# An attention and GLU block rewritten: row-tiled scores, column-tiled values, exponentials shared with VectorE, and a list-scheduled order

## Chip, core and metric

The kernel runs on one core of a Trainium2 chip. The metric is the device time of one execution in microseconds (us), measured on the chip; a profile of one such execution gives the traces quoted below. Before the change the median of two runs was 1394.49 us (1393.20 to 1395.78). Five engines matter: TensorE (PE, its weight loads PEld), ScalarE (ACT), VectorE (DVE), GpSimd (POOL) and SyncE (SP), which only issues DMA here. The record sorts runs into a fast and a slow state (slow: over 1.5% above the fastest run of the same kernel).

## The reference, cut to what matters

```python
# S = 2048 rows, D = 640, H = 32 heads of Dh = 20, F = 1728, all bf16
h  = x + attention(layernorm(x)) @ wo        # softmax over 2048 keys, no mask
h2 = h + ((layernorm(h) @ w_gate) * (layernorm(h) @ w_up)) @ w_down
```

Attention needs 32 x 2048 x 2048 exponentials, which is 1,048,576 per partition of a 128-partition engine. A head has only 20 features. So a score matmul contracts over 20 of the 128 rows that its tile takes in the kernel before (the traces list the tile as 128*128 there), and a value matmul fills only some 20 of its 128 columns.

## The kernel before

It ran in three stages, one after the other: LayerNorm and projections; attention, head by head; then wo, the second LayerNorm and the GLU. The core of the attention loop (cuts marked):

```python
for h in range(H):
    for qh in range(QH):                       # two halves of 1024 queries
        acc = acps.tile([P, QW], F32, name="acc")          # one accumulator (bufs=1)
        for kt in range(NT):                   # 16 blocks of 128 keys
            scr_ = scps.tile([P, QW], F32, name="sc")
            for c in range(QW // 512):
                nc.tensor.matmul(scr_[:, c*512:(c+1)*512],
                                 lhsT=kpad[:, kt*P:(kt+1)*P],   # 20 rows of keys, 108 of zeros
                                 rhs=qpad[:, c*512:(c+1)*512], start=True, stop=True)
            E = epool.tile([P, QW], BF16, name="E")
            nc.scalar.activation(E[:], scr_[:], ACT.Exp, scale=sm_scale)
            for c in range(QW // 512):
                nc.tensor.matmul(acc[:, c*512:(c+1)*512],
                                 lhsT=vext[kt][:, vb:vb+P],     # 20 value columns, ones, padding
                                 rhs=E[:, c*512:(c+1)*512], start=(kt == 0), stop=(kt == NT-1))
        # ... cut: eviction of acc, the sums to DRAM and back, scaling ...
```

The softmax here doesn't subtract the row's maximum and nothing guards it: scores larger than these inputs give would overflow.

## Time and profile before

| stage | us of the span | what fills it |
|---|---|---|
| before the first exponential | 0 to 119 | loads, LayerNorm, projections |
| attention | 119 to 1131 | ScalarE and TensorE, both nearly full |
| after the last exponential | 1131 to 1393 | wo, LayerNorm, GLU on TensorE |

These are lines of the profile page of the kernel before: busy time by engine, the chain of work that ended last, and the two costliest groups (line, engine, operation, tiles, shapes, count, then busy us and mean ns of one, then the engine's idle time before them and its releaser).

```profile
span 1392.9 us, 15855 instructions
PE 1248.1 (90%) x5704; PEld 533.9 (38%) x5704; DVE 372.0 (27%) x593; ACT 1031.3 (74%) x1235; POOL 186.5 (13%) x228
ACT 62%; PE 20%; issue 8%; DMA 4%; DVE 4%; SPq 2%; POOL 0%; ACTq 0%; DVEq 0%
...
L355 ACT ACTIVATE E<-sc 128x1024 bf16<-128x1024 f32 x1024 | 945.8, 1070 | 66.7 <-PE acc L357 66.7
L347 PE MATMUL sc<-qpad,kpad 128*128 128x512 bf16 x2048 | 611.8, 379 | 22.5 <-ACT E L355 20.5
```

The chain is 62% ScalarE, nearly all exponentials. The 66.7 us of idle time before them are the changes of head: a new unit must wait until the one accumulator has been evicted.

The chain in order of time, in the kernel before, shows the pitch (start, duration, what):

```profile
133.26 0.87 ACT E L355
134.12 0.05 issue
134.17 0.87 ACT E L355
135.04 0.05 issue
```

One exponential of 1024 columns starts every 0.91 us. TensorE spends four 512-column matmuls on it. The timeline of the kernel before shows how closely matmuls follow each other:

```profile
1340.12 0.38 PE L514 MATMUL psy<-Wd_9630,hh_10968 128*128 128x512 bf16 x1
1340.33 0.22 PE L521 MATMUL psy<-Wd_9630,hh_10968 128*128 128x128 bf16 x1
```

A 512-column matmul lasts 0.38 us, but the next one starts after 0.21 us (5153 times at full clock in this trace: 215 ns both at the least and in the median). So four take 0.86 us and TensorE is almost as full as ScalarE. A busy share from the 0.38 us would overstate it: one reads TensorE by starts, not by durations.

### The profile page before, as it was taken

What the parts mean: (1) busy time and instruction counts of PE and PEld (TensorE: products, weight loads), DVE (VectorE), ACT (ScalarE), POOL (GpSimd) and SP (SyncE); (2) the same over time, 40 slices, a digit from 0 to 9 for tenths busy, and PEclk for the clock granted to TensorE, in tenths of its full rate; (3) what the DMA queues carried; (4) which work ended last, traced back from release to release, by engine and by line L of the source; (5) the groups of instructions that cost most, each with busy time, mean ns of one, the idle gap of its engine ahead of it and who ended that gap; (6) DMA issues with size and microseconds to landing.
All of it is one profiled execution on the core that took longest, in us unless ns stands there. A gap on an engine that the chain in (4) does not pass through costs nothing.

```text
span 1392.9 us, 15855 instructions
## 1 busy us (share of the span) xinstructions
PE 1248.1 (90%) x5704; PEld 533.9 (38%) x5704; DVE 372.0 (27%) x593; ACT 1031.3 (74%) x1235; POOL 186.5 (13%) x228
## 2 busy tenths in 40 slices
PE   3888999999999999999999999999999953999998
PEld 2433333333333333333333333333333321444443
DVE  8342000420230132004102300410143226453422
ACT  5405999999999999999999999999999941221311
POOL 4223111111111111121111111112111000000000
PEclk9998999999999999999999999999999987999999
DMA  6752000100010001001000100100010144211100
GB/s 164 59 113 48 9 8 8 31 18 9 8 37 8 11 20 25 8 8 33 17 8 9 37 10 8 25 20 8 13 35 10 43 139 129 68 61 40 38 20 19
DMA packets 106258, 48.18 MB, mean 35 GB/s; under 512 B 85956, under 2 KB 97156, under 8 KB 106180
## 3 DMA queue, kind: packets, MB, share of 16 engines
q1 hardware_dynamic: 100088, 39.53, 11.9%
q0 software_dynamic: 4960, 5.78, 2.8%
q10 hardware_dynamic: 1132, 1.87, 0.6%
q8 instruction: 45, 0.74, 0.2%
q14 instruction: 33, 0.27, 0.1%
HBM read 20.40 MB, written 5.51 MB: 19 GB/s over the span
## 4 chain that ended last, share of the span: by engine, by line
ACT 62%; PE 20%; issue 8%; DMA 4%; DVE 4%; SPq 2%; POOL 0%; ACTq 0%; DVEq 0%
ACT E L355 61%; PE psg L494 4%; PE psu L485 4%; PE psy L514 4%; PE acc L357 2%; PE sc L347 2%; DVE qtmp L220 1%; PE psy L521 1%; PE psqk L212 1%; SPq L233 1%; PE psoA L454 1%; PE psv L182 1%; DVE rc L284 0%; SPq L442 0%; DVE lnstats L84 0%
## 5 line engine op out<-in xcount | busy, mean ns | idle before, releaser
L355 ACT ACTIVATE E<-sc 128x1024 bf16<-128x1024 f32 x1024 | 945.8, 1070 | 66.7 <-PE acc L357 66.7
L347 PE MATMUL sc<-qpad,kpad 128*128 128x512 bf16 x2048 | 611.8, 379 | 22.5 <-ACT E L355 20.5
L347 PEld LDWEIGHTS <-kpad 128*128 128x128 bf16 x2048 | 196.5, 96 | 251.9 <-issue 15.7
L365 DVE COPY cst<-acc 52x1024 f32<-52x1024 f32 x64 | 77.9, 1217 | 743.0 <-PE acc L357 743.0
L502 ACT COPY gsb<-psg 128x512 f32<-128x512 f32 (+1 forms) x56 | 32.8, 586 | 107.6 <-PE psg L494 107.4
L329 POOL MEMSET qpad<- 128x1024 bf16 x64 | 60.9, 952 | 358.2 <-issue 358.2
L325 POOL MEMSET kpad<- 128x2048 bf16 x32 | 57.8, 1805 | 369.1 <-PE sc L347 346.7
L357 PE MATMUL acc<-E,vx_102 128*128 128x512 bf16 x128 | 38.4, 381 | 37.7 <-ACT E L355 37.7
L284 DVE RECIPROCAL rc<-Dcol 8x1024 f32<-8x1024 f32 (+1 forms) x9 | 58.9, 6544 | 18.9 <-DMA Dcol<-cst 18.9
L355 ACT ACT_TABLE_LOAD x1 | 1.3, 1283 | 55.4 <-PE sc L347 55.4
L357 PE MATMUL acc<-E,vx_100 128*128 128x512 bf16 x128 | 38.3, 381 | 1.5 <-ACT E L355 1.5
L357 PE MATMUL acc<-E,vx_101 128*128 128x512 bf16 x128 | 38.5, 383 | 0.0
L357 PE MATMUL acc<-E,vx_114 128*128 128x512 bf16 x128 | 37.9, 377 | 0.3 <-ACT E L355 0.3
L357 PE MATMUL acc<-E,vx_115 128*128 128x512 bf16 x128 | 37.9, 377 | 0.3 <-ACT E L355 0.3
L357 PE MATMUL acc<-E,vx_103 128*128 128x512 bf16 x128 | 37.9, 377 | 0.0
L357 PE MATMUL acc<-E,vx_107 128*128 128x512 bf16 x128 | 37.9, 377 | 0.0
L357 PE MATMUL acc<-E,vx_109 128*128 128x512 bf16 x128 | 37.9, 377 | 0.0
L357 PE MATMUL acc<-E,vx_110 128*128 128x512 bf16 x128 | 37.9, 377 | 0.0
L357 PE MATMUL acc<-E,vx_106 128*128 128x512 bf16 x128 | 37.9, 377 | 0.0
L357 PE MATMUL acc<-E,vx_108 128*128 128x512 bf16 x128 | 37.9, 377 | 0.0
L357 PE MATMUL acc<-E,vx_111 128*128 128x512 bf16 x128 | 37.9, 377 | 0.0
L357 PE MATMUL acc<-E,vx_113 128*128 128x512 bf16 x128 | 37.9, 377 | 0.0
(808 smaller groups left out, 1383.3 us busy)
## 6 DMA issues: line engine op xcount, KB each, us to landing
rbt<-rscr SPq DMA_DIRECT2D x64, 80.0 KB
out_dram<-ot SPq DMA_DIRECT2D x16, 160.0 KB
Dcol<-cst SPq DMA_DIRECT2D x64, 4.0 KB
on_70<-cst POOLq DMA_DIRECT2D x16, 40.0 KB, 2.1
on_71<-cst POOLq DMA_DIRECT2D x16, 40.0 KB, 2.1
on_72<-cst POOLq DMA_DIRECT2D x16, 40.0 KB, 2.1
on_73<-cst POOLq DMA_DIRECT2D x16, 40.0 KB, 2.1
qT_85<-qtmp POOLq DMA_DIRECT2D x6, 80.0 KB, 3.1
```

The source lines that it names most:

```text
L182: nc.tensor.matmul(ps[:, 0:512], lhsT=lnT[c][:, t * P:(t + 1) * P], rhs=Wv[c][:, 0:512], start=(c == 0), stop=(c == KT - 1),)
L284: nc.vector.reciprocal(rc[r0:r0 + bs_, :], Dcol[r0:r0 + bs_, :])
L325: nc.gpsimd.memset(kpad[:], 0.0)
L329: nc.gpsimd.memset(qpad[:], 0.0)
L347: nc.tensor.matmul(scr_[:, c * 512:(c + 1) * 512], lhsT=kpad[:, kt * P:(kt + 1) * P], rhs=qpad[:, c * 512:(c + 1) * 512], start=True, stop ...
L355: nc.scalar.activation(E[:], scr_[:], ACT.Exp, scale=sm_scale)
L357: nc.tensor.matmul(acc[:, c * 512:(c + 1) * 512], lhsT=vext[kt][:, vb:vb + P], rhs=E[:, c * 512:(c + 1) * 512], start=(kt == 0), stop=(kt ...
L365: nc.vector.tensor_copy(cst[0:52, :], acc[0:52, :])
L485: nc.tensor.matmul(psu[0:M, :], lhsT=Wu[c][:, f * P:f * P + M], rhs=ln2T[c][:, ch * 512:(ch + 1) * 512], start=(c == 0), stop=(c == KT - 1),)
L494: nc.tensor.matmul(psg[0:M, :], lhsT=Wg[c][:, f * P:f * P + M], rhs=ln2T[c][:, ch * 512:(ch + 1) * 512], start=(c == 0), stop=(c == KT - 1),)
L502: nc.scalar.copy(gsb[0:M, :], psg[0:M, :])
L514: nc.tensor.matmul(psy[:, 0:512], lhsT=hh[f][0:K, tt * P:(tt + 1) * P], rhs=Wd[f][0:K, 0:512], start=(f == 0), stop=(f == NFT - 1),)
```

## The change

The intent is to remove both limits and the serial stages:

1. Scores use 32-row tiles. Four heads lie on partitions 0, 32, 64 and 96, and their four matmuls are meant to run at the same time.
2. Values use 32-column tiles in the same way: four heads accumulate into four quarters of one tile of 512 columns in PSUM, the pool that the kernel's matmuls write to (such a tile is called a bank here).
3. About 18% of the exponentials move to VectorE. It computes `A*s + B` into uint16, and the bits, read as bf16, are a piecewise-linear exponential. Three more copies shifted by constants (27, 55, 94) even out the error. The value matmul adds up all four, so each such block costs four value matmuls.
4. The order of every instruction comes from a list scheduler in the kernel's own Python: projections, wo and GLU ("background jobs") go into the gaps of attention. The order of each engine's instructions is then part of the program.

```diff
-                        nc.tensor.matmul(scr_[...], lhsT=kpad[:, kt*P:(kt+1)*P], rhs=qpad[...], start=True, stop=True)
+                    nc.tensor.matmul(bank[:, n * cw:(n + 1) * cw],
+                                     lhsT=KTt[32 * j:32 * j + Dh, g, kt * P:(kt + 1) * P],
+                                     rhs=QTt[32 * j:32 * j + Dh, g, 0:cw], start=True, stop=True, ...)
-                            lhsT=vext[kt][:, vb:vb + P],
+            nc.tensor.matmul(ACC[32 * j:32 * j + 32, 0:cw], lhsT=VX[:, kt, h * VS:h * VS + 32], rhs=ap,
+                             start=(n == 0), stop=last, tile_position=(0, 32 * j), ...)
-                    nc.scalar.activation(E[:], scr_[:], ACT.Exp, scale=sm_scale)
+                nc.scalar.activation(st["e"][eslot["i"]][:, 0:n * 512], src[:, 0:n * 512], ACT.Exp, scale=SCALE)
+            p_ = add("DVE", ..., lambda e: nc.vector.tensor_scalar(
+                YT[ys["i"]][:, 0, :], bank, scalar1=EXP_A, scalar2=EXP_B, op0=ALU.mult, op1=ALU.add), ...)
+            s1 = s_op(1, 0, SH[1], "DVE", [p_])
+            s2 = s_op(2, 0, SH[2], "DVE", [p_])
+            s3 = s_op(3, 2, SH[3] - SH[2], "POOL", [s2])
+    NON = 10                                         # slots for attention outputs, 8 per chunk of queries
+    CHUNKS = [(0, 512), (512, 512), (1024, 512), (1536, 256), (1792, 256)]
+            mu = add("POOL", ..., lambda e: nc.gpsimd.tensor_tensor(
+                ON[:, on_of[ci, g], 0:cw], a[:, 0:cw], BC[0][:, 0:cw], ALU.mult), ..., gate=lambda: bool(on_free) and ...)
# ... cut: LayerNorm, jobs, the scheduler's loop (some 900 lines) ...
```

## The prediction

> What bounds it now. The span is 1392.9 us. The chain that ended last is 62% ScalarE exponentials, and the ScalarE timeline shows three stages: about 118 us before the first exponential, 1045 us of attention, and about 230 us of output projection and GLU after it. In attention an exponential (128x1024) lasts 1.07 us and starts every 0.917 us, about 0.064 us more than its 1024 columns at 0.833 ns. Every 16 of them cost another 1 to 2 us where the single accumulator waits for its eviction (the waits view: 66.7 us of ScalarE idle for acc). TensorE is almost as full: four 512-column matmuls per exponential, issued about 0.216 us apart, use only 20 of 128 rows (scores) or 52 of 128 columns (values). VectorE is 27% and GpSimd 13% busy.
>
> What changes, with counts from the ordered instruction streams:
> - ScalarE keeps 859,000 of 1,049,000 exponential columns per partition, in 672 instructions of mostly 1536 or 1024 columns. At 0.833 ns plus 0.064 us each that is about 760 us, down from 945 busy.
> - The other 18% go to VectorE as 370 PSUM passes (a 512-column PSUM cast lasts 0.68 us in this trace) and 740 bf16-sized SBUF adds (about 0.2 us, from 0.30 us start to start for the 640-column subtraction), plus 370 adds on GpSimd. VectorE then totals about 600 us: not a bound.[...]
> - TensorE. [...]tiled work (scores 437, values 674, q/k 171 us) would fall to a quarter, 320 us, at perfect four-way overlap; I allow 360, as many score bursts hold only two or three row tiles. Untiled work (values projection, dense q, wo, GLU) is about 250 us. The stream changes tiling mode 1586 times[...]. A 512-column matmul lasts 0.38 us against 0.216 pitch[...]. Sum: 785 to 870 us.
> - Projections, wo and GLU, serial today (about 350 us outside attention), move into gaps inside attention. Outside remain a head of about 25 us (loads, first LayerNorm) and a tail of about 55 us after the last value matmul (243 GLU, 112 down, 32 wo matmuls, one LayerNorm with its transposes).
>
> Critical path. TensorE (about 830 us) and ScalarE (about 760 us) are nearly balanced, and TensorE idles for about 30 us in head and tail. With some 5% lost to waits between them I expect 905 us, a gain of 35%. The range is 850 to 985 us. Chances: faster 0.985, same 0.01, slower 0.005.
>
> What would show it. Right: first exponential before 35 us; ScalarE busy about 800 us (durations overlap), idle mainly waiting for TensorE scores; the chain led by TensorE with ScalarE second; VectorE about 65%; last exponential to end about 60 us; granted clock near 1.0. Wrong: ScalarE above 93% busy during attention ([...]the time nearer 850), or TensorE packed while score or value matmuls of different tiles start more than 0.08 us apart (tiling overlaps worse, time over 950).
>
> What would make it wrong: [...]weight loads of 32-column tiles not hidden; 256-column tiled matmuls limited by issue; VectorE and GpSimd blocking each other so that their share of scores arrives late[...]; the granted clock falling.

Its TensorE sum came to 785 to 870 us: 360 for tiled work, about 250 for untiled work and 175 to 260 for the 1586 mode changes. That last term was the estimate of 0.11 to 0.16 us a change, whose upper figure is the duration of 0.38 us less the pitch of 0.216. The streaming terms count 2.4 columns per ns; the measured 512 columns in 215 ns are 2.38. The 0.833 ns per column of an exponential could not be read from the kernel before, where all exponentials have 1024 columns; the changed kernel's trace gives it (1536 and 1024 columns start 1.331 and 0.904 us apart).

## The result, and the profile after

The changed kernel took 978.91 us, the median of two runs (973.92 and 983.91), and 982.50 us (four runs, 976.87 to 988.34) when it was run again with later experiments (e5). The ratio to the kernel before is 0.702 (95% interval 0.694 to 0.711). Ratios here are the mean time of one kernel's fast runs over that of the other's of the same rounds, so they are not quite the ratios of the medians quoted.

The same parts of the page for the changed kernel, with the rows of 40 equal slices (each digit is a busy share in tenths; PEclk is the granted TensorE clock):

```profile
span 972.1 us, 23682 instructions
PE 865.9 (89%) x9543; PEld 384.7 (40%) x9543; DVE 663.7 (68%) x1743; ACT 782.2 (80%) x727; POOL 288.1 (30%) x419
PE   0889888898999799999999999999999999678968
ACT  0679789696899799999999999999999999306501
PEclk9999999897999899999999999999999999979989
PE 59%; ACT 20%; DVE 11%; issue 6%; DMA 3%; SPq 0%; POOL 0%; ACTq 0%; DVEq 0%; POOLq 0%
...
L932 ACT ACTIVATE EA<-SA 128x1536 bf16<-128x1536 f32 x340 | 505.8, 1488 | 58.5 <-PE D L858 29.9
L932 ACT ACTIVATE EB<-SB 128x1024 bf16<-128x1024 f32 x332 | 354.0, 1066 | 49.2 <-PE ACC L998 47.2
L952 DVE TENSOR_SCALAR Y<-D 128x512 uint16<-128x512 f32 x370 | 254.2, 688 | 145.2 <-PE SA L858 90.4
L962 DVE TENSOR_SCALAR Y<-Y 128x512 uint16<-128x512 uint16 x740 | 199.6, 307 | 6.9
```

ScalarE's exponentials went from 945.8 us busy to about 860 by durations, of which some overlap. The chain is led by TensorE now. The ACT row shows three parts: slices 2 to 14 with 6 to 9 tenths, a stretch from slice 15 to 34 at nine tenths throughout, and then a hole (a 3 and a 0) followed by a short second burst. The waits view of the changed kernel (engine and line, whom it waited for: us in total, times, longest us) says what the hole is:

```profile
ACT EB L932 <- PE ACC L998: 47.2, 1, 47.2
POOL ON L1043 <- PE D L605: 45.9, 1, 45.9
ACT EA L932 <- PE D L858: 29.9, 15, 6.6
ACT EA L932 <- PE SA L858: 26.5, 24, 4.9
```

One ScalarE wait alone is 47.2 us, and one GpSimd wait 45.9 us. In the timeline (start, us, engine, line) the two lie in the same place:

```profile
833.91 1.51 ACT L932 ACTIVATE EA<-SA 128x1536 bf16<-128x1536 f32 x1
882.66 1.02 ACT L932 ACTIVATE EB<-SB 128x1024 bf16<-128x1024 f32 x1 [47.23 <-PE ACC L998]
...
879.36 0.73 POOL L1043 TENSOR_TENSOR ON<-acs,bc 128x256 bf16<-128x256 f32 x1 [45.88 <-PE D L605]
...
854.15 2.29 PE L675 MATMUL D<-L,R 128*128 128x256 bf16 x10 [0.97 <-DVE HH L688]
857.42 2.29 PE L675 MATMUL D<-L,R 128*64 128x256 bf16 x10 [0.97 <-DVE HH L688]
860.67 4.00 PE L704 MATMUL D<-R,HH 128*128 128x320 bf16 x14 [0.96 <-DVE HH L688]
```

It reads as a chain. Normalised outputs go into a ring of ten slots (ON), of which each chunk of queries takes eight. The last chunk found two free. Its third group's multiplication on GpSimd waited for a slot, and a slot comes free only after the wo matmuls (L605) of the chunk before. Those were queued behind the second half of a GLU. Without the multiplication, the accumulator's copies were not released, so no value matmul ran, the exponential buffers stayed full and ScalarE stopped. In the hole TensorE ran only background work, that GLU and then the wo matmuls, one PSUM bank at a time: in the GLU 2.29 us of matmuls, then 0.97 us of waiting for VectorE. The granted clock was 0.50 from 850 to 860 us.

### Where TensorE's time goes

From the starts of all matmuls I worked out an account. Each counts as streaming its columns at 2.4 per ns (measured: matmuls of 512 columns start 215 ns apart, of 256 columns 108, so 2.38 and 2.37), matmuls that overlap in different tiles count once, a gap of up to 0.105 us at a change of tiling mode counts as the change (from 400 to 600 us its medians are 96 to 109 ns), and the rest is idle. What a halved clock costs falls under idle too. It is bookkeeping, so it adds up to the span by itself. What it is good for is comparing kernels.

| us | scores | values | q/k tiles | untiled | mode changes (number) | idle | span of the profiled run |
|---|---|---|---|---|---|---|---|
| changed kernel | 153 | 199 | 45 | 258 | 159 (1586) | 154 | 972 |
| e1, half slots | 153 | 199 | 45 | 257 | 160 (1591) | 144 | 961 |
| e6, wo first | 153 | 198 | 45 | 257 | 160 (1592) | 131 | 947 |
| e7, two banks | 157 | 198 | 45 | 257 | 162 (1609) | 111 | 931 |
| e10, mended | 154 | 199 | 45 | 257 | 158 (1576) | 95 | 911 |
| e11, mended, two patterns | 159 | 152 | 44 | 257 | 162 (1604) | 127 | 904 |
| e4, one pattern | 160 | 128 | 45 | 257 | 162 (1603) | 169 | 923 |
| e3, ScalarE alone | 182 | 126 | 45 | 257 | 174 (1720) | 269 | 1056 |

For the changed kernel, work and mode changes come to 814 us. Idle time is 39 us before 100 us of the span, 50 from 100 to 400, only 22 from 400 to 800, 31 from 800 to 900 (the hole) and 12 in the tail.

The share of the halved clock can be estimated from the trace: half of the time for which matmuls stream, at half rate, inside its windows. The rate is measured: at a granted 0.50, matmuls of 512 columns start 427 ns apart (median of 22 in the kernel before, against 215), and ten 256-column matmuls of the GLU take 2.29 us, against 1.25 just before the clock fell (845.40 us in the changed kernel). That is about 23 us of the 154 in the changed kernel (61 us of halved clock), 17 in e6, 5 in e7, 10 in e10, 40 in e11 and 49 in e4.

A similar count for ScalarE, from the pitch of its exponentials: against 0.833 ns per column and 0.06 us per instruction back to back (exponentials of 1536 and 1024 columns start 1.331 and 0.904 us apart in its tightest stretches, which makes 0.833 ns a column and 0.05 us besides; the account takes 0.06), it lost 48 us from 100 to 400 us of the span, 11 from 400 to 800 and 50 from 800 to 900. The first exponential began at 33.4 us, and the last ended 63 us before the end; these two stretches are called head and tail below.

### The profile page after: what moved, and what is told of

Its sections match the earlier page's. It is cut to its first block, busy times and chain, and to the rows that moved or that the text cites. A ratio compares the mean times of both kernels' runs of the same rounds, so it can differ in the third digit from the quotient of the medians.

```text
span 972.1 us, 23682 instructions
## 1 busy us (share of the span) xinstructions
PE 865.9 (89%) x9543; PEld 384.7 (40%) x9543; DVE 663.7 (68%) x1743; ACT 782.2 (80%) x727; POOL 288.1 (30%) x419
## 4 chain that ended last, share of the span: by engine, by line
PE 59%; ACT 20%; DVE 11%; issue 6%; DMA 3%; SPq 0%; POOL 0%; ACTq 0%; DVEq 0%; POOLq 0%
PE ACC L998 15%; PE D L675 12%; ACT EB L932 10%; ACT EA L932 9%; PE D L704 7%; PE SA L858 7%; PE SB L858 6%; PE D L484 4%; PE D L605 3%; DVE Y L952 3%; PE D L858 2%; PE D L515 2%; PE D L498 1%; DVE HH L688 1%; DVE Y L962 1%
## 5 line engine op out<-in xcount | busy, mean ns | idle before, releaser
L932 ACT ACTIVATE EA<-SA 128x1536 bf16<-128x1536 f32 x340 | 505.8, 1488 | 58.5 <-PE D L858 29.9
L960 POOL TENSOR_SCALAR Y<-Y 128x512 uint16<-128x512 uint16 x370 | 231.8, 627 | 570.8 <-DVE Y L962 376.4
L932 ACT ACTIVATE EB<-SB 128x1024 bf16<-128x1024 f32 x332 | 354.0, 1066 | 49.2 <-PE ACC L998 47.2
L952 DVE TENSOR_SCALAR Y<-D 128x512 uint16<-128x512 f32 x370 | 254.2, 688 | 145.2 <-PE SA L858 90.4
L998 PE MATMUL ACC<-Y,VX 128*32 128x512 bf16 (+1 forms) x1872 | 236.2, 348 | 4.2 <-DVE acs L1026 3.5
L998 PE MATMUL ACC<-EA,VX 128*32 128x512 bf16 (+1 forms) x1265 | 218.5, 353 | 0.0
L962 DVE TENSOR_SCALAR Y<-Y 128x512 uint16<-128x512 uint16 x740 | 199.6, 307 | 6.9
L675 PE MATMUL D<-L,R 128*128 128x256 bf16 (+1 forms) x1100 | 165.0, 282 | 22.4 <-DVE HH L688 13.8
L998 PE MATMUL ACC<-EB,VX 128*32 128x512 bf16 (+1 forms) x827 | 181.1, 350 | 0.0
L858 PE MATMUL D<-QT,KTt 20*128 20x512 bf16 (+1 forms) x468 | 143.2, 340 | 6.9 <-DVE KTt L310 5.6
L1043 POOL TENSOR_TENSOR ON<-acs,bc 128x512 bf16<-128x512 f32 (+1 forms) x40 | 42.5, 1062 | 63.9 <-PE D L605 45.9
```

The costliest lines, as they stand in the source:

```text
L675: nc.tensor.matmul(bank[0:M, off:off + 256], lhsT=w[:, c, f * P:f * P + M], rhs=L2[:, c, :], start=(c == 0), stop=(c == KT - 1), skip_grou ...
L858: nc.tensor.matmul(bank[:, n * cw:(n + 1) * cw], lhsT=KTt[32 * j:32 * j + Dh, g, kt * P:(kt + 1) * P], rhs=QTt[32 * j:32 * j + Dh, g, 0:cw ...
L932: nc.scalar.activation(st["e"][eslot["i"]][:, 0:n * 512], src[:, 0:n * 512], ACT.Exp, scale=SCALE)
L952: p_ = add("DVE", c_psum(512), lambda e: nc.vector.tensor_scalar(YT[ys["i"]][:, 0, :], bank, scalar1=EXP_A, scalar2=EXP_B, op0=ALU.mult, o ...
L960: nc.gpsimd.tensor_scalar(y[:, dst, :], y[:, src_, :], scalar1=float(d), scalar2=1.0, op0=ALU.add, op1=ALU.mult)
L962: nc.vector.tensor_scalar(y[:, dst, :], y[:, src_, :], scalar1=float(d), scalar2=None, op0=ALU.add)
```

## Experiments

The theory after reading the trace: TensorE's total carries the time; ScalarE is full as well from 400 to 800 us; and the difference from the prediction is idle time with three causes, namely the ring, late projections and the head. The rival: ScalarE alone carries it, so that its 47 us hole is worth 47 us, and TensorE's work is of no weight.

| run | median us of the fast runs (number) | ratio to before | what it does |
|---|---|---|---|
| e5 after again | 982.50 (4) | 0.705 | nothing |
| e1 half slots | 963.23 (4) | 0.691 | 256-row chunks take half a slot |
| e2 head memsets | 974.72 (4) | 0.699 | memsets out of the head |
| e3 no vector exp | 1054.51 (3 of 4) | 0.756 | all exponentials on ScalarE |
| e4 one pattern | 925.83 (3 of 4) | 0.667 | one bit pattern, not four |
| e6 wo first | 951.52 (4) | 0.683 | wo ahead of the older GLU |
| e7 two banks | 933.31 (4) | 0.670 | two background banks during projections |
| e8 serial columns | 1154.83 (1, state unknown) | | values head by head, planned so |
| e9 regrouped | 973.80 (4) | 0.699 | values head by head, plan unchanged |
| e10 mended | 909.45 (4) | 0.651 | e2 + e6 + e7, bursts of four |
| e11 mended, two patterns | 906.70 (4) | 0.651 | e10, two bit patterns |

All gave results that agree with the reference within its tolerance.

### e5: the changed kernel again

> The changed kernel, untouched, in the rounds of the next three, because its own time rests on two runs (974 and 984 us). 970 to 985 us if those two were typical. The profiled execution tells whether the same ScalarE hole near 840 us comes back (it must, since the order is fixed) and whether the windows of halved TensorE clock fall at other places.

Nothing was edited. 982.50 us is inside the expectation. The hole came back to the tenth of a microsecond (47.2 and 45.9 us), so it belongs to the order. The windows of halved clock (61 us in all in the first trace, 65 in this one) came back in part: from 780 us on they have the same lengths and start some 3 us later, as the first exponential does, while before 400 us they differ. In the first trace they last 3.41, 6.83 or, once, 17.07 us; what brings them about, no run here settles. The variation of 1% between runs goes with the clock: three of this kernel's six runs took 974 to 977 us at a mean clock of 0.967 or 0.968, and three 984 to 988 us at 0.949 to 0.958.

### e1: half slots

```diff
-                ON[:, on_of[ci, g], 0:cw], a[:, 0:cw], ...
+                ON[:, on_of[ci, g][0], on_of[ci, g][1]:on_of[ci, g][1] + cw], a[:, 0:cw], ...
-                gate=lambda: bool(on_free) and ...
+                gate=lambda: (bool(on_free) or cw == 256 and bool(on_half)) and ...
```

> Attention outputs of the 256-row chunks take half a slot of the ring of ten, so no group of the last chunk has to wait for the wo matmuls of the chunk before. Ring theory: the 47 us in which ScalarE has no exponential (834 to 883 us of the changed kernel's trace) and the 45.9 us wait of GpSimd for a wo matmul vanish. If ScalarE alone carries the time, the kernel gains nearly all of it, 40 to 47 us. If TensorE carries it, the GLU work of that stretch has to be done elsewhere and only TensorE's own waits there are won, about 27 us of its 154 in all: a gain of 15 to 30 us. If the hole is only the list scheduler's choice to do GLU first, it stays and nothing is gained.

Both long waits are gone from the waits view, so the ring theory holds. The last exponential ended at 867 us and not at 909. But the tail grew from 63 to 94 us, and the kernel gained 2.0% against e5 (0.691 over 0.705, 19 us) and not 47 us. The GLU that had filled the hole ran after attention in place of during it. TensorE's idle time fell from 154 to 144 us. This speaks for TensorE's total and against the rival: ScalarE's idle 47 us were worth 19.

### e6: wo first

```diff
+            if ci == 2:
+                order += half_j[:18] + parts[3][0] + half_j[18:] + parts[3][1]
```

> The ring of ten slots stays as it is, but the wo matmuls of the fourth chunk are queued before the second half of the third chunk's GLU, so that its slots come free sooner. Ring theory: the hole goes by this road too, and, as in e1, the GLU work moves behind the last exponential, so that 10 to 20 us are won and not 47. If e1's gain came from anything else in the half slots, this one gains nothing.

The hole went by this road too. 951.52 us is 31 us less than e5, more than the 10 to 20 expected; its tail grew too, to 84 us. It beats e1, and TensorE's idle time from 800 to 900 us is 5 us, against 17 in e1 and 31 in the changed kernel. The clock differs there as well (not halved in e6, 12 us in e1, 20 in the changed kernel), so how much of the 12 us between e1 and e6 is the order alone was not separated.

### e7: two banks for background jobs during projections

```diff
-   if bank_use["D"][i] is None and (bgs == 0 or not attn["started"] or ...):
+   if bank_use["D"][i] is None and (bgs == 0 or proj_over.done is None and exps == 0 or not attn["started"] or ...):
```

> While projections are still to be done, background jobs may hold both spare PSUM banks and not only one. TensorE waits about 50 us between 100 and 400 us of the changed kernel, and ScalarE loses 48 us against back to back there, mostly at the changes of head group, where the keys of the next group are late. If one bank is what makes the projections late, ScalarE's loss in that stretch falls below 35 us and the kernel gains 10 to 20 us. If it is TensorE's capacity, nothing changes beyond 5 us.

49 us were won, over twice the upper figure. ScalarE's loss between 100 and 400 us fell from 48 to 11 us, and TensorE's idle time there from 50 to 14. The direction is what the one-bank theory says. The hole is still in this plan (39.0 us in the waits view). The busy time from 100 to 400 us in the windows view (window, its length, then busy us of PE, PEld, DVE, ACT, POOL with counts, granted clock, DMA share, GB/s), first of the changed kernel:

```profile
100.00:400.00 300.00, 270.60 (x2738) 99.98 (x2730) 204.13 (x514) 256.45 (x229) 88.05 (x130) 0.95 0.16 47
```

and of e7:

```profile
100.00:400.00 300.00, 293.72 (x3058) 111.43 (x3064) 226.03 (x586) 291.94 (x263) 100.39 (x148) 1.00 0.18 53
```

With one bank, a projection had to wait for the eviction of the one before (0.69 us on VectorE plus the hand-over). The keys of the next group of heads came late, and ScalarE waited up to 6.6 us at a time. The size is not the bank's alone: the clock rose from 0.95 to 1.00 in this stretch as well, and by the estimate above the halved clock took some 17 us less of TensorE's time than in the changed kernel. All four runs of e7 had a mean clock of 0.985 to 0.996 and all six of the changed kernel 0.949 to 0.968, so the clock goes with the plan; what brings it about was not tested.

### e2: memsets out of the head

```diff
-        for t in range(0, NT, 4):
-            nc.gpsimd.memset(VX[:, t:t + 4, :], 1.0)
-        nc.gpsimd.memset(WO[:], 0.0)
+        nc.vector.memset(ones[:, :, :, Dh:VS], 1.0)
+        # ... and the padding; WO is zeroed on GpSimd after the last transpose
```

> The GpSimd memsets of the first 16 us go: VectorE writes only the columns of ones that are needed (about 1 us, at a time when it idles), and the zeroing of the wo tile comes after the last LayerNorm transpose. [...]the two tiny VectorE casts that took 3.1 and 4.3 us in the head (128x8 and 128x4) fall under 0.3 us, the first exponential starts 5 to 7 us earlier than 33.4 us, and the whole gains about that, under 1%. Rival: those casts are slow because of something else at the start (a load, a first use), then nothing moves.

In the timeline of the changed kernel, two tiny VectorE instructions are slow while GpSimd's memsets run (0.73 to 14.4 us):

```profile
6.94 3.12 DVE L395 CAST lb<-lmv 128x8 bf16<-128x8 f32 x1
10.10 4.29 DVE L396 TENSOR_SCALAR lb<-lb 128x4 bf16<-128x4 bf16 x1
...
0.73 9.31 POOL L337 MEMSET VX<- 128x2732 bf16 x4 [0.29 <-POOLq L1271]
9.97 4.39 POOL L338 MEMSET WO<- 128x5120 bf16 x1
```

The same two in e2:

```profile
7.47 0.17 DVE L398 CAST lb<-lmv 128x8 bf16<-128x8 f32 x1
7.68 0.17 DVE L399 TENSOR_SCALAR lb<-lb 128x4 bf16<-128x4 bf16 x1
```

Each ended with the end of a memset before, within 0.03 us, and both take 0.17 us now. So by e2 the memsets held them up; by what means, no trace shows. The first exponential began 5.7 us earlier (27.7 us). The total is not separable from noise: the interval of e2's ratio (0.697 to 0.702) touches that of e5 (0.701 to 0.710), and this profiled run had 90 us of halved clock, 41 of them from 800 to 900 us, around the hole.

### e3: all exponentials on ScalarE

```diff
         def take_for_dve(used):
+            return None
```

> VectorE takes no exponentials; all 1,048,576 columns go to ScalarE in about 820 instructions. ScalarE theory: 874 + 50 us of exponentials back to back, plus head 33, tail 63 and about 60 to 110 of waits: 1030 to 1130 us, so the VectorE share is worth 60 us or more. TensorE theory: TensorE loses 1404 value matmuls (three extra pieces for each VectorE block, about 60 us of streaming at fourfold overlap) and is not hurt otherwise: 920 to 980 us.

1054.51 us, inside the ScalarE theory's 1030 to 1130: VectorE's share is worth about 72 us against e5. TensorE lost 73 us of value streaming here, and the time rose all the same. So ScalarE is the tighter engine once it has all the exponentials. The windows view of e3 shows it, in a stretch in which the clock was halved throughout:

```profile
439.00:541.00 102.00, 85.83 (x449) 18.85 (x448) 3.33 (x7) 99.56 (x88) 5.07 (x4) 0.50 0.07 21
```

TensorE, at half clock, was recorded busy for 85.83 of 102 us, and ScalarE still for 99.56. This run had 314 us of halved clock.

### e4: one bit pattern

```diff
-SH = (0, 27, 55, 94)
+SH = (0,)
-            for q, o in enumerate((p_, s1, s2, s3)):
+            for q, o in enumerate((p_,)):
```

> Each VectorE block is one bf16 bit pattern in place of the sum of four (less exact on purpose): 923 to 1404 fewer value matmuls, 740 fewer VectorE adds, 370 fewer GpSimd adds, the same exponentials on ScalarE and the same 1590 or so mode changes. TensorE theory: 40 to 60 us less streaming shows as 35 to 60 us less time, about 920 to 940 us. ScalarE theory: ScalarE's work is unchanged, so the time falls by under 15 us.

The three fast runs took 925.21, 925.83 and 937.16 us, by the ratios about 53 us less than e5 (0.667 against 0.705), though ScalarE's work did not change. That is what the TensorE theory says (920 to 940), and the rival allowed under 15. It is cheaper arithmetic and less exact, so it is a probe and not a proposal. Value streaming fell by 71 us. ScalarE's loss between 100 and 400 us fell to 14 us with nothing done to the banks, so more than one thing relieves that stretch. From 400 to 800 us it did not fall (22 us, against 11), but 85 us of that stretch were at halved clock, against 3.

Two things keep this from being a clean test. The probe also took 740 adds from VectorE (199.6 us busy in the changed kernel) and 370 from GpSimd, and VectorE empties the banks of the projections: TensorE's streaming and earlier evictions are not told apart. And the clock was halved for 126 us in all.

### e8 and e9: does the order of the heads matter?

In e8, four value matmuls of one head were emitted before those of the next, with the scheduler aware of it:

```diff
+                    for j in range(4):
+                        for _ in range(min(c[j], 4)):
+                            emit_piece(j)
```

> The same value matmuls, but up to four of one head are issued one after another before those of the next head[...]. If the overlap comes from neighbours with different tiles, value matmuls of 512 columns start about 0.21 us apart within a head, their streaming grows from 199 us to 500 us or more, and the kernel takes 1200 to 1350 us. If the array overlaps them whatever the order, the time stays within 5% of 979 us.

1154.83 us missed the range, and the mechanism was wrong as well: value streaming grew to 254 us only, not to 500. Most of the added time is idle time of TensorE (over 300 us by the same account), in a worse plan: the waits view shows GpSimd waiting once for 116.4 us at the ring. The clock was halved for 346 us, for which no cause was tested. So the run could not answer the question, and e9 kept the plan:

```diff
+            burst.append((j, lambda: nc.tensor.matmul(ACC[32 * j:32 * j + 32, 0:cw], ...)))
+                    for _, f in sorted(burst, key=lambda b: b[0]):
+                        f()
```

> e8 changed the plan as well as the order, since the list scheduler knew of the slower order. Here the plan is that of the changed kernel to the last instruction, and only inside each burst of up to sixteen value matmuls are they emitted head by head. If TensorE lets matmuls of different column tiles pass one another, a burst of sixteen still spans about 0.7 us from first start to last, and the time stays within 2% of the 982 us of e5. If it starts them strictly in order, sixteen span 2.6 us or more, streaming of the values goes from 199 to over 450 us, and the kernel takes over 1150 us.

973.80 us, the same as the changed kernel, and values stream for 203 us. This is one burst of sixteen in the timeline of e9, emitted as four of head 0, four of head 1, and so on (rows merge neighbours with the same source):

```profile
255.68 0.42 PE L999 MATMUL ACC<-Y,VX 128*32 128x512 bf16 x3
255.72 0.57 PE L999 MATMUL ACC<-EB,VX 128*32 128x512 bf16 x2
255.92 0.38 PE L999 MATMUL ACC<-EA,VX 128*32 128x512 bf16 x1
...
256.37 0.38 PE L999 MATMUL ACC<-Y,VX 128*32 128x512 bf16 x1
256.38 0.38 PE L999 MATMUL ACC<-EB,VX 128*32 128x512 bf16 x1
```

Its sixteen starts are 0, 14, 27, 40, 227, 241, 255, 269, 443, ... 700 ns. Four start 13 to 14 ns apart, then nothing for the length of a stream, then four more. The median over 17 such bursts is 699 ns from first start to last, against 669 ns in the changed kernel, where the four heads alternate and start 2 to 5 ns apart (in the burst shown below). Strict order would need an estimated 2.6 us: twelve pitches of 0.215 us, three within each head. So the matmuls do not start in the order of emission: those of one head are passed by later ones of other heads, which are for other column tiles. The first four to start stand up to twelve matmuls apart in the order of emission. The trace doesn't name the tile of a matmul, but it names the sources. This is the start of the same burst in the changed kernel, which emits the heads in turn:

```profile
257.44 0.40 PE L998 MATMUL ACC<-Y,VX 128*32 128x512 bf16 x3
257.45 0.60 PE L998 MATMUL ACC<-EB,VX 128*32 128x512 bf16 x2
257.67 0.38 PE L998 MATMUL ACC<-EA,VX 128*32 128x512 bf16 x1
```

In all 17 bursts the sources (Y, EA, EB) start in the same order in both kernels; in 15 of them the order in which e9 emits is a different one.

### e10 and e11: the mended kernel

e10 is e2, e6 and e7 together, with `AVMIN = 4` for 3 (a burst of values waits for four pieces of every head; what this alone is worth was not run); the arithmetic is that of the changed kernel.

> e2, e6 and e7 together, and a burst of values waits for four pieces of every head, not three; the arithmetic is that of the changed kernel. TensorE theory: streamed columns and mode changes stay at about 815 us, and the idle time falls from 155 us to about 85 to 95 (e7's 110, less some 25 for the hole and 5 for the head): 900 to 920 us. If ScalarE carried the time, the hole (47 us), the late projections (40 us) and the head (6 us) would add up to 885 to 892 us.

909.45 us (904.15 to 912.93), 35% less than before and 7.7% less than the changed kernel (0.651 over 0.705). It beats both kernels. It lies in the range of the TensorE theory (900 to 920) and above the rival's (885 to 892). From its page:

```profile
span 911.0 us, 23716 instructions
PE 845.2 (93%) x9549; PEld 377.4 (41%) x9555; DVE 652.5 (72%) x1753; ACT 784.0 (86%) x734; POOL 284.2 (31%) x420
ACT  0689999999998999999999999999899999993201
PEclk9999999999999999999999999999799999999979
```

There is no hole, and ScalarE is near nine tenths from slice 4 on. Its tail is longer, 86 us after the last exponential.

> e10 with two bit patterns in place of four for each VectorE block: about 900 value matmuls fewer, some 45 us of streaming. TensorE theory: 860 to 885 us if the clock stays whole. In e4, with one pattern, 126 us fell in windows of halved clock and ate about half of the gain; if less work for TensorE brings those windows here too, 875 to 900 us. ScalarE theory: within 10 us of e10.

906.70 us, the same as e10 (both ratios 0.651). The rival's expectation is met in number and neither of the TensorE theory's is: 47 us of value streaming were saved, and idle time rose by 32. But the clock did not stay whole: it was halved for 102 us, against 28 in e10. The clock row of e11's page:

```profile
PEclk9999999999889999997599999996699979999989
```

By the estimate given with the account, the halved clock cost TensorE 40 us here and 10 in e10, which is nearly all of the added idle time. ScalarE's chain is much the same in both: in e11 27 us of head, 757 of exponentials, 45 of waits and 76 of tail. So TensorE's time, halved clock included, hardly changed, nor did ScalarE's work, and e11 does not tell which of the two carries the mended kernel. That stays open.

## Why the prediction was right or wrong

The measured 979 us lies in the stated range (850 to 985), near its upper end: two of the kernel's six runs (987.83 and 988.34 us) lie above it. Faster was given 0.985. The expected value, 905 us, was 74 us low.

- *TensorE's sum of 785 to 870 us.* Right in sum, 814, in part by luck, since its terms erred both ways (they count columns at 2.4 per ns; the measured pitch of 215 ns for 512 gives 2.38). Tiled work took 397 us and not 360, since many bursts hold two or three tiles. The 1586 mode changes took 159 us and not 175 to 260. The trace gives the price: from 400 to 600 us (411 changes), medians of 96 to 109 ns beyond the streaming of the last matmul for the six pairs of modes (row tiles, column tiles, whole array). What the array does at a change, no trace shows. My estimate from the 0.38 us duration was up to 60% too high.
- *ScalarE about 760 us.* Right: 756 us back to back, 782 busy by the page against "about 800".
- *Head of 25 us, first exponential before 35.* 33.4 us. The head was 8 us longer than the sum had it, and e2 shows 6 of them: two VectorE instructions held up until GpSimd's memsets ended (3.12 and 4.29 us, 0.17 each without the memsets). The prediction named this contention as a risk, but for the exponentials, where it cost little (the adds' median is 286 ns, the 95th percentile 296, and 27 of 740 took over 400 ns). The list scheduler also avoids planning these adds of the two engines at the same time, so the contention was not put to the test there.
- *Tail of 55 us.* 63 us.
- *"With some 5% lost to waits."* This is the step that failed: idle time of TensorE was put at about 30 us in head and tail and 43 us elsewhere, 73 in all, and was 154. Some 23 us of that are the halved clock, which the prediction set at nothing ("near 1.0"). For the rest it was mis-sized because I took the waits as a general loss of a balanced pair, and the two that counted were particular ones in the fixed order. Mending the ring of ten slots won 19 us in e1 and 31 in e6 (idle time down by 10 and 23 in the traces). Mending the single background bank during projections won 49 us (e7, idle time down by 43, some 17 of it halved clock). With both mended, the head as well and bursts of four, e10 takes 909 us with 95 us idle. That this lies so near the predicted 905 is partly luck, as the terms of TensorE's sum show.
- *Balanced engines.* Right, with a nuance that the prediction lacked: which of the two is tighter differs by stretch. From 100 to 400 us TensorE and the projections hold ScalarE up (it loses 48 us, and 14 and 11 in e4 and e7); from 400 to 800 us ScalarE is the fuller one (it loses 11 us of 400, TensorE 22).
- *Signs.* VectorE about 65%: 68%. Chain led by TensorE, ScalarE second: 59% and 20%. Clock near 1.0: 0.968. "ScalarE above 93% busy during attention" as the sign of a time near 850 was a poor one: ScalarE stood at 98% from 400 to 800 us (393.94 of 400), but the rest of attention did not follow.

## What to carry to other kernels

When two engines are nearly balanced and the order is fixed, look for single long waits in the plan rather than for a percentage: one wait of 47 us was a buffer ring whose release sat behind unrelated work in a queue. The hole in one engine was not worth its length here, because work that another engine did in it had to go somewhere else (47 us of hole on ScalarE; 19 us won in e1, 31 in e6; TensorE idled 31 us there). A probe that takes work from one engine and leaves the other untouched (e4, e11) helps to tell which of them carries the time, but first see what else it relieves (e4 freed VectorE as well) and what the granted clock did: in e11 the halved clock (102 us, against 28 in e10) took back, by the estimate above, 30 of the 47 us of streaming that the probe saved.
